# Moving the loads of four input sets into the second FFT stage, returning the filter taps in four parts, and re-ordering a weight conversion

## The chip, the cores and the metric

One core of a Trainium2 chip runs the whole kernel. The metric is the time of one execution on the device, in microseconds; the time before is the median of three runs. The engines are PE (TensorE matmul, with its weight loads PEld), DVE (VectorE), ACT (ScalarE), POOL (GpSimd) and SP (SyncE), which here issues every DMA.

## The reference

Three layers follow one another on 12480 tokens of 128 channels. The first is a long convolution in the sequence with a generated filter, gated by x; the second and third are feed-forward layers of width 2048.

```
h = (relu(pos_emb @ w1) @ w2) * exp(-0.01 * pos)     # filter taps, 12480 x 128
u = x * v
y = irfft(rfft(u, 2S) * rfft(h, 2S))[:S]             # causal convolution, every channel
x1 = x * y
h1 = x1 @ w_in                                       # 128 -> 2048
x2 = (P(h1) / (Q(h1) + 1e-6)) @ w_out                # P cubic, Q quadratic in h1
out = leaky_relu(x2 @ w2_in) @ w2_out
```

The weights of the two feed-forward layers (`ws`, four matrices) come as 64-bit floats and are converted on the chip.

## The kernel before, in words

The transform of length 2S is done in two stages of matmuls (a split of the index by 128), for two groups of 64 channels, g = 0 and 1. The kernel goes through these stages in order; every engine gets its instructions in the order of the Python text, and works them off in that order.

1. The filter net (`layer1`, `layer2`) makes the taps: those of group 0 stay in `hf` (a part of the tile `wk`), those of group 1 go to a DRAM buffer `hsc`.
2. The first stage of group 0: 16 steps `first(0, 1, i)` on the taps, then 16 steps `first(0, 0, i)` on u. Each step is 16 matmuls (L555) into one of three PSUM buffers (`bank_b`), and one ACT copy into `A` (L561).
3. The second stage of group 0, `second_stage(0)`: NB = 23 blocks, each with a table of 256 KB from DRAM (`c_m`, L570, four buffers `mt`, loaded three blocks ahead). A block is 8 forward matmuls (`xp`, L587), an ACT copy (L589), two DVE products (L596), two DVE sums (L602, L603), and, three blocks later, 8 inverse matmuls (`gp`, L622), an ACT copy (L635) into one of two `gs` buffers and a store to the DRAM buffer `bd` (L642). The last three inverse halves alternate with the first steps of the next stage.
4. The first stage of group 1: 16 steps on u, 16 on the taps, which are read back from `hsc` into `hf` (L313, L315).
5. The second stage of group 1, where POOL does the sums.
6. The two-layer part: 26 tiles of tokens, in an order that a planner writes out (`plan`); every matrix product of both layers and of the last transform step is in it.

u is made in 16 sets of 8 channels, sets 0 to 7 for group 0, 8 to 15 for group 1. `load_x` puts x of a set at u's own place, `load_v` puts v into one of four buffers `VS`, and `make_u` multiplies (L398) and forms sum and difference (L400), then issues the loads of v four sets on and of x six sets on. Two sets are made in stage 1, twelve in stage 2, two in stage 3 (blocks 0 and 2).

The conversion of the weights goes through 16 pieces of 512 columns (`conv_w`), 512 KB of DRAM each, with two buffers `raw`, which lie where two of the `VS` buffers were. It is a generator: `feed(n)` issues the next n steps, one DVE instruction each. A piece has six steps (L506 exponent, L509 sign, L512 mantissa, L517 low word, L521 sign and exponent merged, L525 product) and, for the first eight pieces, a seventh (L533, the low part of a split, after ACT's L530 has made the high part). ACT's Relu on the exponent (L507) is issued right behind L506. With the sixth step the load of the piece two on is issued (L494). 28 steps fall in stage 3 (from block 4 on), 64 in stage 4, the rest in stage 5. The loads of pieces 0 and 1 stand between stages 2 and 3.

All DMAs go through SP's one queue in the order of the text; an issue whose buffer isn't free holds up what is behind it.

Of the kernel before, what the change touches and what calls it, by code (L numbers as in the profile page):

```python
# [10 lines left out]
F32 = mybir.dt.float32  # L11
F32R = mybir.dt.float32r
# [282 lines left out]
def conv_moe_moe(ctx: ExitStack, tc: tile.TileContext, I, out, dbg=None):  # L295
# [13 lines left out]
    def spread(eng, dst, src):  # L309

        n = dst.shape[0]
        m = n // 16 * 16
        eng.dma_start(dst[:m], src[:m])  # L313
        if m < n:
            eng.dma_start(dst[m:], src[m:])  # L315

    with tc.manual_schedule():
# [61 lines left out]
        VB = 4  # L379
        VS = [cut(wk, N2 * DG + i * 2 * DS * 64, [DS, 2, N2 // 2]) for i in range(VB)]  # L380
        pool.memset(cone, C1)

        act.activation(pars[:, 6:7], cone, AF.Abs_reciprocal_sqrt)
# [3 lines left out]
        def load_x(c):  # L387
            if c < NG * NS:
                sp.dma_start(u[c // NS][:96, c % NS], I["xu"][c, :96])

        def load_v(c):
            if c < NG * NS:
                spread(sp, VS[c % VB][:NU], I["vu"][c])

        def make_u(c):

            t, w = u[c // NS][:NU, c % NS], VS[c % VB][:NU]
            dve.tensor_tensor(out=w, in0=w, in1=t, op=ALU.mult)  # L398
            for q, alu in ((0, ALU.add), (1, ALU.subtract)):
                dve.tensor_tensor(out=t[:, :, q], in0=w[:, :, 1], in1=w[:, :, 0], op=alu)  # L400
            load_v(c + VB)
            load_x(c + VB + 2)

        sp.dma_start(w1b, I["w1b"])
        for a, b in zip(PJ, PJ[1:]):
# [93 lines left out]
        def conv_w(c):  # L499
            k, q = divmod(c, NQ)  # L500
            l, sl = k % 2, slice(q * QW, (q + 1) * QW)
            raw = raws.pop(c)
            hi, lo = raw[:, :, 1], raw[:, :, 0]
            ex, sc = (view(t, [QW], I32) for t in ("ex", "sc"))
            w = view("w", [QW]) if k < 2 else uw[:, l * FF + q * QW : l * FF + (q + 1) * QW]
            dve.tensor_scalar(out=ex, in0=hi, scalar1=0x7FF00000, scalar2=None, op0=ALU.bitwise_and)  # L506
            act.activation(ex, ex, AF.Relu, bias=-float(896 << 20))  # L507
            yield
            dve.tensor_scalar(out=sc, in0=hi, scalar1=-0x80000000, scalar2=None, op0=ALU.bitwise_and)  # L509
            yield  # L510

            dve.tensor_scalar(  # L512
                out=hi, in0=hi, scalar1=0xFFFFF, scalar2=0x100000, op0=ALU.bitwise_and, op1=ALU.bitwise_or
            )
            yield
            w0 = hi.bitcast(F32)
            dve.scalar_tensor_tensor(  # L517
                out=w0, in0=lo.bitcast(U32), scalar=2.0**-32, in1=hi, op0=ALU.mult, op1=ALU.add
            )
            yield  # L520
            dve.scalar_tensor_tensor(  # L521
                out=sc, in0=ex, scalar=3, in1=sc, op0=ALU.logical_shift_left, op1=ALU.bitwise_or
            )
            yield
            dve.scalar_tensor_tensor(  # L525
                out=w, in0=w0, scalar=-(2.0**-20) if k == 2 else 2.0**-20, in1=sc.bitcast(F32), op0=ALU.mult, op1=ALU.mult
            )
            load_w(c + 2)
            if k < 2:
                act.copy(wh[l][:, sl], w)  # L530
            yield
            if k < 2:
                dve.tensor_tensor(out=wl[l][:, sl], in0=w, in1=wh[l][:, sl].bitcast(F32), op=ALU.subtract)  # L533
                yield

        def conv_all():
            for c in range(4 * NQ):
# [137 lines left out]
        for i in range(16):  # L675
            first(0, 0, i)
            if i < 3:
                run(st, 1)
            if i in (1, 4, 7, 10, 13):
                make_u(uc)  # L680
                uc += 1
        load_w(0)
        load_w(1)
        ustack.close()
        wpool = ctx.enter_context(tc.tile_pool(name="wpool", bufs=1, side="right", reuse_waits="tile"))
        wh = [wpool.tile([128, FF], F32R, name=f"wh{l}") for l in range(2)]
        wl = [wpool.tile([128, FF], F32R, name=f"wl{l}") for l in range(2)]
        for b in range(NB):
            run(st, 1)
            if b in (0, 2):  # L690
                make_u(uc)
                uc += 1
            if b > 3:
                feed(1 + b % 2)
        for i in range(16):
            first(1, 0, i)
            if i < 3:
                run(st, 1)
            elif i == 3:
                for c in range(0, DG, 16):  # L700
                    spread(sp, hf[:NH, c : c + 16], hsc[:, c : c + 16])
            feed(2)
        for i in range(16):
            first(1, 1, i)
# [21 lines left out]
        for b in range(NB + 3):  # L726
            run(st, 1)
            feed(1)
            if b == 17:
# [2 lines left out]
                sp.dma_start(xt0, I["xm"][:, : COLS[0]])  # L732
                load_b(bt0, 0, 0, TILES[0])
        run(st, 1)
        fstack.close()


# [274 lines left out]
```

## Time and profile before

| | |
|---|---|
| median of three runs | 1588.57 us (1585.23 to 1590.54) |
| the profiled execution | 1586.99 us, span 1585.2 us |
| mean granted TensorE clock | 0.987 |
| PE busy | 1539.4 us, 97% |
| DVE, ACT, POOL busy | 1422.8, 1315.2, 1279.8 us |
| DMA | 88.86 MB, mean 56 GB/s |

The page's slices, 40 of 39.6 us each, show where the engines are not full: the first eight slices, that is the stages 1 to 5, and the start of the last part in them.

```profile
PE   7989799799999999999999999999999999999999
DVE  6577577599999999999999999999999999999992
ACT  5523543388999999999999999999999999999995
POOL 5000037488999999999999999999999999999993
PEclk9999899699999999999999999999999999999999
DMA  8954655684011110111101000000000000000000
```

A digit is the busy share of a slice in tenths; PEclk is the granted clock in tenths of full speed, DMA the mean busy share of the 16 DMA engines.

### The profile page before, as it was taken

What the parts mean: (1) busy time and instruction counts of PE and PEld (TensorE: products, weight loads), DVE (VectorE), ACT (ScalarE), POOL (GpSimd) and SP (SyncE); (2) the same over time, 40 slices, a digit from 0 to 9 for tenths busy, and PEclk for the clock granted to TensorE, in tenths of its full rate; (3) what the DMA queues carried; (4) which work ended last, traced back from release to release, by engine and by line L of the source; (5) the groups of instructions that cost most, each with busy time, mean ns of one, the idle gap of its engine ahead of it and who ended that gap; (6) DMA issues with size and microseconds to landing.
All of it is one profiled execution on the core that took longest, in us unless ns stands there. A gap on an engine that the chain in (4) does not pass through costs nothing.

```text
span 1585.2 us, 21639 instructions
## 1 busy us (share of the span) xinstructions
PE 1539.4 (97%) x6782; PEld 1078.3 (68%) x6782; DVE 1422.8 (90%) x2426; ACT 1315.2 (83%) x2532; POOL 1279.8 (81%) x1098
## 2 busy tenths in 40 slices
PE   7989799799999999999999999999999999999999
PEld 5878688687666666666666666666666666666665
DVE  6577577599999999999999999999999999999992
ACT  5523543388999999999999999999999999999995
POOL 5000037488999999999999999999999999999993
PEclk9999899699999999999999999999999999999999
DMA  8954655684011110111101000000000000000000
GB/s 242 255 166 152 175 171 177 155 175 100 5 34 34 28 34 7 34 34 28 34 7 34 13 14 1 13 13 13 13 7 7 14 7 7 7 7 1 8 7 13
DMA packets 79849, 88.86 MB, mean 56 GB/s; under 512 B 51745, under 2 KB 59651, under 8 KB 79079
## 3 DMA queue, kind: packets, MB, share of 16 engines
q1 hardware_dynamic: 79734, 87.49, 20.2%
q8 instruction: 53, 0.87, 0.2%
q14 instruction: 62, 0.50, 0.1%
HBM read 66.59 MB, written 20.88 MB: 55 GB/s over the span
## 4 chain that ended last, share of the span: by engine, by line
PE 58%; POOL 18%; DVE 10%; DMA 7%; ACT 4%; issue 3%; SPq 0%; POOLq 0%; ACTq 0%; DVEq 0%
PE o1p L864 13%; PE o2p L864 9%; POOL wk L900 8%; PE h L424 7%; PE h L425 7%; PE h L426 7%; PE yP L818 3%; PE xp L587 3%; POOL wk L891 3%; POOL wk L893 3%; DMA wk<-vu 3%; DVE v L902 2%; PE gp L622 2%; DVE g L915 2%; DVE wk L897 2%
## 5 line engine op out<-in xcount | busy, mean ns | idle before, releaser
L900 POOL TENSOR_TENSOR wk<-wk 128x972 f32<-128x972 f32 (+2 forms) x208 | 470.5, 2262 | 40.7 <-DVE wk L897 29.7
L864 PE MATMUL o1p<-g,u 128*128 128x486 f32 (+2 forms) x832 | 384.1, 570 | 1.4 <-DVE g L915 1.1
L891 POOL TENSOR_SCALAR wk<-wk,pars 128x486 f32<-128x486 f32 (+2 forms) x416 | 314.4, 756 | 21.0 <-ACT wk L883 19.6
L902 DVE SCALAR_TENSOR_TENSOR v<-wk,absb,v 128x486 f32<-128x486 f32 (+2 forms) x416 | 297.1, 714 | 8.1 <-ACT v L885 7.5
L864 PE MATMUL o2p<-wk,u 128*128 128x486 f32 (+2 forms) x624 | 297.3, 565 | 0.0
L909 DVE SCALAR_TENSOR_TENSOR v<-v,u 128x486 f32<-128x486 f32 (+2 forms) x416 | 273.6, 658 | 12.8 <-ACT u L907 11.7
L885 ACT ACTIVATE v<-h,absb 128x486 f32<-128x486 f32 (+2 forms) x416 | 262.8, 645 | 20.0 <-DVE g L915 17.6
L897 DVE TENSOR_TENSOR wk<-h,wk 128x486 f32<-128x486 f32 (+2 forms) x416 | 270.7, 651 | 1.6 <-POOL wk L891 0.7
L912 DVE SCALAR_TENSOR_TENSOR v<-v,u 128x486 f32<-128x486 f32 (+2 forms) x416 | 262.1, 658 | 2.5
L915 DVE TENSOR_TENSOR g<-wk,v 128x486 f32<-128x486 f32 (+2 forms) x416 | 256.2, 648 | 8.1 <-POOL wk L900 6.7
L907 ACT ACTIVATE u<-u 128x486 f32<-128x486 f32 (+2 forms) x416 | 254.8, 613 | 6.9
L922 ACT ACTIVATE wk<-h 128x486 f32<-128x486 f32 (+2 forms) x416 | 239.2, 576 | 23.5 <-PE h L426 12.7
L905 ACT ACTIVATE u<-v 128x486 f32<-128x486 f32 (+2 forms) x416 | 238.2, 573 | 20.1 <-DVE v L902 12.9
L424 PE MATMUL h<-zh,wh 128*128 128x486 f32 (+2 forms) x416 | 247.1, 594 | 4.5 <-ACT rh L924 3.1
L883 ACT ACTIVATE wk<-h 128x486 f32<-128x486 f32 (+2 forms) x416 | 238.7, 574 | 10.8 <-PE h L426 7.8
L893 POOL TENSOR_SCALAR wk<-wk,pars 128x972 f32<-128x972 f32 (+2 forms) x208 | 239.4, 1151 | 0.0
L424 PE MATMUL h<-uh,wh 128*128 128x486 f32 (+2 forms) x416 | 231.7, 557 | 0.7 <-DVE wk L897 0.7
L864 PEld LDWEIGHTS o1p<-g,u 128*128 128x128 f32 x832 | 153.0, 189 | 93.6 <-issue 37.2
L602 POOL TENSOR_TENSOR wk<-wk 128x256 f32<-128x256 f32 x22 | 18.2, 828 | 204.6 <-DVE wk L596 199.5
L425 PE MATMUL h<-zl,wh 128*128 128x486 f32 (+2 forms) x416 | 159.7, 384 | 0.0
L426 PE MATMUL h<-zh,wl 128*128 128x486 f32 (+2 forms) x416 | 159.2, 383 | 0.0
L425 PE MATMUL h<-ul,wh 128*128 128x486 f32 (+2 forms) x416 | 158.7, 381 | 0.0
(86 smaller groups left out, 2309.9 us busy)
## 6 DMA issues: line engine op xcount, KB each, us to landing
bd<-wk SPq DMA_DIRECT2D x44, 256.0 KB
bt<-bd SPq DMA_DIRECT2D x100, 112.5 KB
wk<-c_m SPq DMA_DIRECT2D x43, 256.0 KB
dt<-c_d SPq DMA_DIRECT2D x25, 344.5 KB
wk<-ws SPq DMA_DIRECT2D x16, 512.0 KB
u<-xu SPq DMA_DIRECT2D x16, 384.0 KB
wk<-vu SPq DMA_DIRECT2D x16, 384.0 KB
xt<-xm SPq DMA_DIRECT2D x13, 243.0 KB
```

The source lines that it names most:

```text
L424: pe.matmul(dst, w_h, z_h, start=start, stop=False)
L425: pe.matmul(dst, w_h, z_l, start=False, stop=False)
L426: pe.matmul(dst, w_l, z_h, start=False, stop=stop)
L864: pe.matmul(o, wo[l][:, f], T.pop((src, n))[:, :w], start=(f == 0), stop=(f == NF - 1))
L885: act.activation(bank("v", n)[:, :w], one("h1"), AF.Abs, scale=kk)
L891: pool.tensor_scalar(out=q, in0=sq, scalar1=a3, scalar2=a1, op0=ALU.mult, op1=ALU.add)
L893: pool.tensor_scalar(out=new("p", n, 2)[:, : 2 * w], in0=T["s", n][:, : 2 * w], scalar1=a2, scalar2=a0, op0=ALU.mult, op1=ALU.add)
L897: dve.tensor_tensor(out=half("nn"), in0=one("h1"), in1=two("q"), op=ALU.mult)
L900: pool.tensor_tensor(out=nn, in0=nn, in1=T["p", n][:, : 2 * w], op=ALU.add)
L902: dve.scalar_tensor_tensor(out=one("v"), in0=two("s"), scalar=bb, in1=one("v"), op0=ALU.mult, op1=ALU.add)
L909: dve.scalar_tensor_tensor(out=one("v"), in0=one("v"), scalar=C1, in1=one("r0"), op0=ALU.add, op1=ALU.mult)
L915: dve.tensor_tensor(out=mk("g"), in0=two("nn"), in1=one("v"), op=ALU.mult)
```

## The change

Only sets 0 to 11 are made before the second stage of group 0. Of the last four sets, x and v load in its blocks 0 to 10, v into two new buffers `VL` (where later the second layer's low weights lie), and u is formed one DVE instruction a block, in blocks 4 to 15. The weights' first two loads are issued in blocks 8 and 9, and the conversion starts at block 11, with one step a block. A conversion piece has five DVE steps and, for the split pieces, a sixth, which is issued inside the next piece; ACT's two steps are issued later too: the Relu behind the second step (on a result of the first), the copy to the high part inside the next piece. The load of the piece two on is issued one step earlier. The taps' return is issued in four parts, at steps 4, 7, 10 and 13 of the first stage of group 1 instead of all at step 3.

```diff
+        def form_u(c):
+            t, w = u[c // NS][:NU, c % NS], v_of(c)
             dve.tensor_tensor(out=w, in0=w, in1=t, op=ALU.mult)
+            yield
             for q, alu in ((0, ALU.add), (1, ALU.subtract)):
                 dve.tensor_tensor(out=t[:, :, q], in0=w[:, :, 1], in1=w[:, :, 0], op=alu)
-            load_v(c + VB)
-            load_x(c + VB + 2)
+                yield
+        def make_u(c):
+            for _ in form_u(c):
+                pass
+            if c + VB < LATE:
+                load_v(c + VB)
+            if c + VB + 2 < LATE:
+                load_x(c + VB + 2)
...
             dve.tensor_scalar(out=ex, in0=hi, scalar1=0x7FF00000, scalar2=None, op0=ALU.bitwise_and)
-            act.activation(ex, ex, AF.Relu, bias=-float(896 << 20))
+            while rest:
+                act.copy(*rest.pop())
             yield
-            dve.tensor_scalar(out=sc, in0=hi, scalar1=-0x80000000, scalar2=None, op0=ALU.bitwise_and)
+            m = w.bitcast(I32)
+            dve.tensor_scalar(
+                out=m, in0=hi, scalar1=0xFFFFF, scalar2=0x100000, op0=ALU.bitwise_and, op1=ALU.bitwise_or
+            )
+            act.activation(sc, ex, AF.Relu, bias=-float(896 << 23), scale=8.0)
             yield
-            dve.tensor_scalar(
-                out=hi, in0=hi, scalar1=0xFFFFF, scalar2=0x100000, op0=ALU.bitwise_and, op1=ALU.bitwise_or
-            )
-            yield
-            w0 = hi.bitcast(F32)
+            while lows:
+                out, a, b = lows.pop()
+                dve.tensor_tensor(out=out, in0=a, in1=b.bitcast(F32), op=ALU.subtract)
+                yield
             dve.scalar_tensor_tensor(
-                out=w0, in0=lo.bitcast(U32), scalar=2.0**-32, in1=hi, op0=ALU.mult, op1=ALU.add
+                out=w, in0=lo.bitcast(U32), scalar=2.0**-32, in1=m, op0=ALU.mult, op1=ALU.add
             )
             yield
             dve.scalar_tensor_tensor(
-                out=sc, in0=ex, scalar=3, in1=sc, op0=ALU.logical_shift_left, op1=ALU.bitwise_or
+                out=sc, in0=hi, scalar=-0x80000000, in1=sc, op0=ALU.bitwise_and, op1=ALU.bitwise_or
             )
+            load_w(c + 2)
             yield
...
-            load_w(c + 2)
             if k < 2:
-                act.copy(wh[l][:, sl], w)
+                rest.append((wh[l][:, sl], w))
+                lows.append((wl[l][:, sl], w, wh[l][:, sl]))
             yield
...
-            if i in (1, 4, 7, 10, 13):
+            if i in (2, 6, 10):
                 make_u(uc)
                 uc += 1
-        load_w(0)
-        load_w(1)
...
+        LOADS = {
+            0: [(load_x, 12)], 1: [(load_v, 12)], 2: [(load_x, 13)], 3: [(load_v, 13)], 4: [(load_x, 14)],
+            5: [(load_x, 15)], 7: [(load_v, 14)], 8: [(load_w, 0)], 9: [(load_w, 1)], 10: [(load_v, 15)],
+        }
+        late = (x for c in range(LATE, NG * NS) for x in form_u(c))
         for b in range(NB):
             run(st, 1)
-            if b in (0, 2):
-                make_u(uc)
-                uc += 1
-            if b > 3:
-                feed(1 + b % 2)
+            for load, c in LOADS.get(b, ()):
+                load(c)
+            if 4 <= b < 16:
+                run(late, 1)
+            if b >= 11:
+                feed(1)
...
-            elif i == 3:
-                for c in range(0, DG, 16):
-                    spread(sp, hf[:NH, c : c + 16], hsc[:, c : c + 16])
+            elif i in (4, 7, 10, 13):
+                c = (i - 4) // 3 * 16
+                spread(sp, hf[:NH, c : c + 16], hsc[:, c : c + 16])
             feed(2)
```

Not shown are the allocations (`VL`, the second layer's low weights in a pool of their own behind it) and a last `feed(100)` after the second stage of group 1.

## Rows read from the trace of the kernel before

**Rows 1.** Busy time by stretch: engines with instructions, granted clock, DMA share, GB/s.
```profile
74.40:91.80 17.40, 11.63 (x41) 9.21 (x42) 14.82 (x24) 2.34 (x4) 0.00 (x0) 0.80 0.71 200
91.80:156.90 65.10, 63.73 (x293) 55.01 (x291) 49.11 (x98) 25.07 (x44) 0.00 (x0) 1.00 0.50 158
...
169.00:215.50 46.50, 38.76 (x465) 34.62 (x464) 30.70 (x58) 27.89 (x42) 0.00 (x0) 0.89 0.67 185
...
293.00:1585.20 1292.20, 1278.80 (x4776) 856.81 (x4776) 1223.05 (x2082) 1187.64 (x2313) 1208.27 (x1012) 0.99 0.11 26
```

**Rows 2.** The chain that ended last: start us, us, what.
```profile
79.13 6.59 DMA wk<-c_m
...
170.44 6.91 DMA wk<-hsc
...
177.42 11.15 DMA wk<-ws
```

**Rows 3.** PE's timeline, 74 to 97 us: start, us, instruction, idle before.
```profile
74.44 3.72 PE L587 MATMUL xp<-A,wk 128*128 128x256 f32 x16 [0.92 <-ACT A L561]
...
85.86 3.75 PE L587 MATMUL xp<-A,wk 128*128 128x256 f32 x8 [4.55 <-DMA wk<-c_m]
...
91.77 1.89 PE L587 MATMUL xp<-A,wk 128*128 128x256 f32 x8
93.50 1.89 PE L622 MATMUL gp<-wk,em 128*128 128x256 f32 x8
95.22 1.89 PE L587 MATMUL xp<-A,wk 128*128 128x256 f32 x8
```

**Rows 4.** PE's timeline, the first stages of both groups and the last block.
```profile
53.83 19.69 PE L555 MATMUL ap<-f,u 98*64 98x180 f32 x256
...
156.06 1.03 PE L587 MATMUL xp<-A,wk 128*128 128x256 f32 x4
...
169.00 13.64 PE L555 MATMUL ap<-f,u 98*64 98x180 f32 x176
190.38 5.07 PE L555 MATMUL ap<-f,u 98*64 98x180 f32 x32 [7.74 <-ACT A L561]
195.23 20.32 PE L555 MATMUL ap<-f1t,wk 128*64 128x180 f32 x256
```

**Rows 5.** SP's timeline, the issue of the first two weight pieces.
```profile
76.15 2.89 SPq L494 DMA_DIRECT2D wk<-ws  x2
```

**Rows 6.** SP's waits, 0 to 220 us: total us, times, longest.
```profile
SPq L494 <- DVE wk L525: 22.7, 6, 4.8
```

**Rows 7.** Busy time by stretch, three stretches with full DMA engines; columns as rows 1.
```profile
50.00:75.00 25.00, 24.09 (x313) 22.24 (x310) 17.64 (x21) 15.19 (x20) 0.00 (x0) 1.00 1.04 246
...
130.00:135.00 5.00, 5.00 (x24) 4.12 (x23) 3.73 (x8) 2.42 (x5) 0.00 (x0) 1.00 0.91 330
175.00:187.00 12.00, 7.64 (x102) 6.88 (x96) 4.52 (x8) 4.44 (x7) 0.00 (x0) 0.97 1.02 225
```

**Rows 8.** Groups of instructions, 74.4 to 216 us: busy us, mean ns, idle before.
```profile
L521 DVE SCALAR_TENSOR_TENSOR wk<-wk 128x512 int32<-128x512 int32 x14 | 9.6, 687 | 3.5 <-ACT wk L507 3.5
...
L507 ACT ACTIVATE wk<-wk 128x512 int32<-128x512 int32 x14 | 8.9, 633 | 12.9 <-DVE wk L506 12.9
...
L509 DVE TENSOR_SCALAR wk<-wk 128x512 int32<-128x512 int32 x14 | 5.9, 421 | 0.0
...
L398 DVE TENSOR_TENSOR wk<-wk,u 98x1024 f32<-98x1024 f32 x3 | 3.7, 1223 | 3.3 <-DMA wk<-vu 3.3
```

**Rows 9.** The page's DMA issues: count, KB each.
```profile
bd<-wk SPq DMA_DIRECT2D x44, 256.0 KB
...
wk<-c_m SPq DMA_DIRECT2D x43, 256.0 KB
...
wk<-ws SPq DMA_DIRECT2D x16, 512.0 KB
...
wk<-vu SPq DMA_DIRECT2D x16, 384.0 KB
...
wk<-hsc SPq DMA_DIRECT2D x4, 640.0 KB
```

More of the change, by code (lines that the diff above doesn't have):

```diff
@@ L378, in conv_moe_moe, with v_of @@
         w2n, w1n = (win[:, : N2 // 2], win[:, N2 // 2 : N2]), win[:, N2:]
-        VB = 4
+        VB, LATE = 4, 12
         VS = [cut(wk, N2 * DG + i * 2 * DS * 64, [DS, 2, N2 // 2]) for i in range(VB)]
+        VL = []
+        def v_of(c):
+            return (VS[c % VB] if c < LATE else VL[c % 2])[:NU]
         pool.memset(cone, C1)
@@ L392, in load_v @@
             if c < NG * NS:
-                spread(sp, VS[c % VB][:NU], I["vu"][c])
-        def make_u(c):
-            t, w = u[c // NS][:NU, c % NS], VS[c % VB][:NU]
+                spread(sp, v_of(c), I["vu"][c])
+        def form_u(c):
+            t, w = u[c // NS][:NU, c % NS], v_of(c)
             dve.tensor_tensor(out=w, in0=w, in1=t, op=ALU.mult)
+            yield
             for q, alu in ((0, ALU.add), (1, ALU.subtract)):
                 dve.tensor_tensor(out=t[:, :, q], in0=w[:, :, 1], in1=w[:, :, 0], op=alu)
-            load_v(c + VB)
-            load_x(c + VB + 2)
+                yield
[6 more added lines that the diff above has]
+                load_x(c + VB + 2)
         sp.dma_start(w1b, I["w1b"])
@@ L521, in conv_w @@
             dve.scalar_tensor_tensor(
-                out=sc, in0=ex, scalar=3, in1=sc, op0=ALU.logical_shift_left, op1=ALU.bitwise_or
+                out=sc, in0=hi, scalar=-0x80000000, in1=sc, op0=ALU.bitwise_and, op1=ALU.bitwise_or
             )
+            load_w(c + 2)
             yield
             dve.scalar_tensor_tensor(
-                out=w, in0=w0, scalar=-(2.0**-20) if k == 2 else 2.0**-20, in1=sc.bitcast(F32), op0=ALU.mult, op1=ALU.mult
+                out=w, in0=w, scalar=-(2.0**-20) if k == 2 else 2.0**-20, in1=sc.bitcast(F32), op0=ALU.mult, op1=ALU.mult
             )
-            load_w(c + 2)
             if k < 2:
-                act.copy(wh[l][:, sl], w)
+                rest.append((wh[l][:, sl], w))
+                lows.append((wl[l][:, sl], w, wh[l][:, sl]))
             yield
-            if k < 2:
-                dve.tensor_tensor(out=wl[l][:, sl], in0=w, in1=wh[l][:, sl].bitcast(F32), op=ALU.subtract)
-                yield
+        rest, lows = [], []
         def conv_all():
@@ L678, in conv_moe_moe @@
                 run(st, 1)
-            if i in (1, 4, 7, 10, 13):
+            if i in (2, 6, 10):
                 make_u(uc)
                 uc += 1
-        load_w(0)
-        load_w(1)
         ustack.close()
+        tstack = ExitStack()
         wpool = ctx.enter_context(tc.tile_pool(name="wpool", bufs=1, side="right", reuse_waits="tile"))
         wh = [wpool.tile([128, FF], F32R, name=f"wh{l}") for l in range(2)]
-        wl = [wpool.tile([128, FF], F32R, name=f"wl{l}") for l in range(2)]
+        wl = [wpool.tile([128, FF], F32R, name="wl0")]
+        vpool = tstack.enter_context(tc.tile_pool(name="vpool", bufs=1, side="right", reuse_waits="tile"))
+        VL += [vpool.tile([128, DS, 2, N2 // 2], F32, name=f"vl{i}") for i in range(2)]
+        assert uc == LATE
+        LOADS = {
[3 more added lines that the diff above has]
+        late = (x for c in range(LATE, NG * NS) for x in form_u(c))
         for b in range(NB):
             run(st, 1)
-            if b in (0, 2):
-                make_u(uc)
-                uc += 1
-            if b > 3:
-                feed(1 + b % 2)
+            for load, c in LOADS.get(b, ()):
[4 more added lines that the diff above has]
+                feed(1)
+        tstack.close()
+        l1pool = ctx.enter_context(tc.tile_pool(name="l1pool", bufs=1, side="right", reuse_waits="tile"))
+        wl.append(l1pool.tile([128, FF], F32R, name="wl1"))
         for i in range(16):
@@ L734, in conv_moe_moe @@
         run(st, 1)
+        feed(100)
         fstack.close()
```

## The prediction

> **What bounds the kernel now.** I read four views, in this order. The stretch table of all engines comes first: it cuts the run at the stages that the kernel's text names. From 293 us on, in the two-layer part, PE is busy 1278.80 of 1292.20 us [rows 1]; the change touches nothing there, so this part only shifts in time. Ahead of it, PE is busy 11.63 of the 17.40 us at the start of the second stage of channel group 0 (74.4 to 91.8), nearly all of 91.8 to 156.9, and 38.76 of 46.50 us in the first stage of group 1 (169 to 215.5). In both of the loose stretches the granted clock is below 1.00 as well, which is time at the lower of its two levels. So the question is what PE waits for at these two places.
>
> The chain of waits answers it, and the reader is to see three entries in it [rows 2]: 6.59 us for a table block (`wk<-c_m`) issued at 79.13, then 6.91 us for hf (`wk<-hsc`) from 170.44, and 11.15 us for a piece of weights (`wk<-ws`) issued at 177.42. All three are transfers on the one SP queue.
>
> PE's own timeline gives sizes [rows 3]. The second stage starts at 74.44 with two blocks at once; the fourth block starts at 85.86, after 4.55 us of idleness that a `c_m` load ended, and its eight matmuls take 3.75 us where eight take 1.89 later: it is the half clock. From 91.77 on a block comes every 95.22 - 91.77 = 3.45 us, half of it the forward matmuls (`xp`) and half the inverse ones (`gp`), eight of one shape each: 1.73 us a half. In the first stage of group 1, PE stops before 190.38 for 7.74 us because ACT doesn't copy, and ACT doesn't copy because its next instruction, the weights' Relu, waits for VectorE, which waits for the weights [rows 2, 4].
>
> The SP issues say why the table block was late: in the queue's order it stands behind x and v of the sets up to 15 and behind two 512 KB weight pieces, which go out from 76.15 on [rows 5], so its own issue is at 79.13 [rows 2].
>
> **The change, part by part.**
>
> *1. Loads of x and v for sets 12 to 15 and of weight pieces 0 and 1 leave the first stage.* That is 4 x (384 + 392) KB + 2 x 512 KB, 4.2 MB (a v load is its 384 KB and a tail of 8 KB) [rows 9]. At the 246 GB/s that the DMA engines gave there at a share of 1.04, that is fully busy [rows 7], it is 17 us of transfers that are no longer ahead of the tables. PE itself is busy 24.09 of 25 us in that stretch, so the end of the first stage at 74.4 doesn't move. Tables 0 to 3 and x of set 12 have nothing to wait for on the queue and land before 74. The stretch from 74.44 to the fifth block then costs three lone `xp` halves, one `xp` with its `gp`: 5 x 1.73 = 8.65 us, and the fifth block starts at 83.1 instead of 91.77. Gain: 91.77 - 74.44 - 8.65 = **8.7 us**. Next late would be table 4, which waits for the first block's matmuls (76.2) and has until 83.1; it needs about 1 us of transfer. Bounds: 8.7 if it is in time, about 5 if tables 4 and 5 come behind x and v at two or so us each.
>
> *2. The same loads, now inside the second stage.* In steps 0 to 10 there is one more transfer in nearly each step. Prices: 256 KB of tables or of stores at 330 GB/s, which a busy share of 0.91 gave, so some 360 at full share [rows 7, 9]; I take 330, 0.79 us. One x or v: 384 KB at 246/1.04 = 237 GB/s, 1.66 us. A weight piece: 1.59 us. Between 76.2 and the end of step 10 (83.1 + 7 x 3.45 = 107.3) the queue carries ten tables and eight stores (18 x 0.79 = 14.2), seven x and v (11.6; x of set 12 is earlier) and two weight pieces (3.2): 29.0 us of work in 31.1 us. It fits, with 7% to spare. Tables have three steps of lead, and a store has until its buffer returns two steps later. SP is blocked less: a weight load waits on VectorE's conversion step that stands behind the whole block, 22.7 us in six times [rows 6], and holds the tables and stores queued after it. Four such loads fell between 91.77 and 156.06, now two do (the other two wait for nothing). From the fifth block to the last at 156.06 there are 18 steps, 62.1 us, so these blocks cost 2.1 us now [rows 3, 4]; I keep half of that and add 0.6 for the fuller queue. Gain: **0.5 us**. Bounds: +2.1 to -4.8 us, the latter if all of it goes at the 237 GB/s of x and v (35.9 us for 31.1).
>
> *3. Forming u of these sets on VectorE in steps 4 to 15.* One instruction a step, 1.22 us the longest [rows 8]. A step has 49.11/65.10 x 3.45 = 2.6 us of VectorE work now, a conversion instruction of about 0.5 in it [rows 1, 8]; with 1.22 in its place some 3.3 us in 3.45; no instruction of the path comes later by more than that 1.2, and a block's PSUM has three buffers. I cost it at nothing; if the cover fails it costs four times about 1 us.
>
> *4. hf comes back in four parts, and weights go between them.* Today 4 x 656 KB (640 and a tail of 16) [rows 9] stand as one lump ahead of a weight piece, hence 11.15 us. From 169.00 to the end of the first stage of group 1 (195.23 + 20.32 = 215.55) PE has 29 steps; sixteen such steps took 19.69 us in group 0, 1.23 each, so it needs 35.7 us, and takes 46.5 [rows 4]. So 10.8 us are lost, 7.74 of them idle and the rest at the half clock. After: every three steps (3.7 us) one part and one weight piece share the queue, (672 + 524) kB at the 225 GB/s of just this mixture [rows 7]: 5.3 us, 1.6 too much, four times 6.4. The first excess is hidden by the two raw buffers, so VectorE comes about 4.5 us late in all, and PE may run two steps (2.5 us) ahead of ACT's copies. I take 2.0 us lost, in small pieces that don't drop the clock. Gain: **8.8 us**. Bounds: 10.8 (nothing late) to 2 (each excess reaches PE, with the clock falling as now).
>
> The Trainium skill's page "SBUF — State Buffer", section "Summary: rules for kernel authors", says to estimate a transfer between HBM and SBUF with about 358 GB/s. By it a part and a weight piece would take 3.3 us and fit their 3.7, and the sum would be 2.0 us better. The row of this very mixture disagrees, 225 GB/s at a share of 1.02 [rows 7].
>
> *5. Conversion.* One VectorE instruction (L509) of 0.42 us a piece goes, 16 in all. The others have the shapes and engines of rows that are there: sign mask and merge as the 0.69 us one, the Relu 0.63 us [rows 8]. None is on PE's path unless its weights are late: the saving is worth nothing by itself. ACT's Relu and copy now wait on VectorE results that are a step old, so that ACT doesn't stand behind VectorE; that is in the sums of 2 and 4. The 12 last conversion steps fall in the second stage of group 1, as before. Its last weight load now waits on VectorE in that stage's first step and holds table 4 there: I take 0, with +-1.5.
>
> **Sum.** 8.7 + 0.5 + 8.8 = 18.0 us. The profiled execution took 1586.99 us with a span of 1585.2; less 18.0 it is 1569.0. The median of the runs shown, 1588.57, lies 1.6 us above that execution, which is inside their own spread of 1585.23 to 1590.54. I forecast 1569.
>
> **Rivals.**
>
> *A. hf still gets in the way.* The wait for weights is spread over four places instead of removed: all 6.4 us reach PE and the clock falls (some 3 us). Loss 9 instead of 2: gain 11, 1576. For it: these transfers fill the queue (1.02). Against: each delay is under two steps. Chance 0.15.
>
> *B. The second stage becomes bound by transfers, mildly.* Part 2 comes to its -4.8 us and part 1 loses 3: gain 5.7 - 4.8 + 8.8 = 9.7, 1577. For: 7% to spare only. Against: lead of three steps. Chance 0.12.
>
> *C. Slower.* The second stage doesn't get beyond the rate that it shows now, 158 GB/s [rows 1]. From 76.2 to its last block, at 146 by my sum, it must carry 19 tables, 23 stores, seven x and v, four weight pieces: 15.8 MB in 70 us, 226 GB/s. At 158 this takes 100 us; 30 lost against 18.0 won, 1599. It decides below 15.8 / (70 + 18) = 180 GB/s, where stores come back too late for the two `gs` buffers, ACT waits and PE behind it. Against it: the 158 come at a share of 0.50 [rows 1], the queue stands idle half of the time. Chance 0.07.
>
> *D. No change.* The same at about 180 GB/s: 1585 to 1592. Chance 0.05.
>
> **How the numbers follow.** The forecast has 0.61, with 1564 to 1574 as its own range (all losses gone: 8.7 + 2.1 + 10.8 + 1.5 = 23.1; at the other end a gain of 13). A and B reach 1577, both together 1581. The range is 1562 to 1581. About 0.3%, 4.8 us, is what a measurement here can tell from no change: faster 0.88 (forecast, A, B), within 0.05 (D), slower 0.07 (C).
>
> **What would show it.** Right: no `c_m` wait of PE between 74 and 92 and the fifth block's `xp` near 83; block step 3.45 to 3.6 us through step 10 with a DMA share near 0.9; the first stage of group 1 in 36 to 39 us with granted clock 1.00; the two-layer part as long as now. Part 1 is wrong if PE waits for a table in steps 3 to 5; part 2 if ACT's copies of `gp` wait for `bd` stores in most steps up to 10; part 4 if VectorE's first conversion instruction waits for `ws` over 2 us at a time and PE behind it. The whole is wrong if the two-layer part changes by over 2 us.

## The result, and the profile after

The changed kernel takes 1575.44 us (median of 8 runs, 1572.51 to 1582.58), the kernel before 1588.57 (8 runs, 1585.23 to 1594.53): ratio 0.9915, interval [0.990, 0.993]. That is 13.1 us won; 18.0 were forecast (1569, range 1562 to 1581). The profiled execution took 1575.34 us, mean granted clock 0.989.

Two rows of the changed kernel's page (span 1573.6 us), in slices of 39.3 us:

```profile
PE   7999999799999999999999999999999999999999
...
PEclk9999999699999999999999999999999999999999
```

PE's third slice (the start of the second stage of group 0) and its fifth (the first stage of group 1) read 9 now, where they read 8 and 7, and the clock's fifth is back at 9 too. The first (the filter net) and the eighth (the start of the two-layer part) stay low. PE's own timeline says where the time went (start in us, duration, instruction, idle before it):

```profile
77.00 7.17 PE L602 MATMUL xp<-A,wk 128*128 128x256 f32 x32 [0.91 <-ACT A L576]
...
85.73 1.89 PE L602 MATMUL xp<-A,wk 128*128 128x256 f32 x8
...
133.80 1.99 PE L637 MATMUL gp<-wk,em 128*128 128x256 f32 x8 [1.28 <-ACT wk L650]
...
149.44 1.03 PE L602 MATMUL xp<-A,wk 128*128 128x256 f32 x4
...
161.33 16.08 PE L570 MATMUL ap<-f,u 98*64 98x180 f32 x208
179.14 2.66 PE L570 MATMUL ap<-f1t,wk 128*64 128x180 f32 x32 [1.73 <-ACT A L576]
...
184.38 2.66 PE L570 MATMUL ap<-f1t,wk 128*64 128x180 f32 x32 [0.93 <-ACT A L576]
...
195.57 6.32 PE L570 MATMUL ap<-f1t,wk 128*64 128x180 f32 x80 [0.78 <-ACT A L576]
202.80 5.45 PE L602 MATMUL xp<-A,u 128*128 128x256 f32 x24 [0.91 <-ACT A L576]
```

The second stage of group 0 opens with 32 `xp` matmuls in a row and no wait for a table: 85.73 - 77.00 = 8.73 us to the fifth block, 91.77 - 74.44 = 17.33 before [rows 3]. The blocks then run at PE's own pace but for one stop of note, before 133.80. In the first stage of group 1 the one long stop of 7.74 us, with the half clock behind it [rows 4], has become five short ones at full clock. The table of stretches (length, then busy time of PE, PEld, DVE, ACT, POOL, granted clock, DMA share, GB/s) shows it as clock and transfer rate:

```profile
77.00:85.70 8.70, 8.70 (x40) 7.69 (x41) 5.74 (x12) 2.35 (x4) 0.00 (x0) 1.00 0.66 202
85.70:149.40 63.70, 62.42 (x289) 54.63 (x289) 52.17 (x98) 22.57 (x39) 0.00 (x0) 1.00 0.61 191
161.30:202.80 41.50, 36.74 (x465) 32.71 (x464) 30.21 (x55) 29.41 (x46) 0.00 (x0) 1.00 0.83 219
...
280.90:1573.60 1292.70, 1280.46 (x4776) 858.44 (x4776) 1223.46 (x2082) 1187.72 (x2313) 1208.14 (x1012) 0.99 0.11 26
```

The clock is 1.00 in the three stretches of the change (0.80, 1.00 and 0.89 before [rows 1]), and the second stage moves 191 GB/s instead of 158. In the first stage of group 1 PE still needs only 36.74 of 41.50 us.

The same cuts of PE's timeline for this kernel and for all kernels below (us, each of one profiled execution; "first": up to the first step on the taps; "st1": the first stage of group 0; "to 5th" and "blocks": its second stage up to the start of the fifth block, and from there to the start of the last; "to u": to the fourth step on u of group 1, the first that no inverse half interrupts; "1st g1": from there to the second stage of group 1; "2nd g1": up to its last inverse half; "to w": to the two-layer part's first matmul; "two-layer": from there to the end):

| kernel | first | st1 | to 5th | blocks | to u | 1st g1 | 2nd g1 | to w | two-layer | span |
|---|---|---|---|---|---|---|---|---|---|---|
| before | 34.26 | 40.18 | 17.33 | 64.29 | 12.94 | 47.41 | 72.75 | 5.85 | 1290.19 | 1585.2 |
| after | 35.33 | 41.67 | 8.73 | 63.71 | 11.89 | 41.47 | 71.40 | 6.69 | 1292.71 | 1573.6 |
| loads_only | 35.30 | 40.18 | 8.74 | 64.55 | 11.86 | 47.00 | 79.64 | 5.86 | 1291.47 | 1584.6 |
| loads_only_28 | 35.16 | 41.73 | 8.73 | 70.11 | 11.86 | 47.57 | 72.12 | 5.92 | 1290.30 | 1583.5 |
| taps_only | 34.77 | 42.17 | 14.99 | 64.51 | 12.93 | 39.39 | 72.76 | 5.88 | 1291.50 | 1578.9 |
| conversion_only | 34.95 | 40.17 | 17.29 | 63.50 | 11.86 | 46.87 | 70.02 | 5.94 | 1295.00 | 1585.6 |
| without_late_loads | 35.04 | 40.17 | 17.85 | 63.57 | 11.85 | 43.12 | 69.97 | 6.65 | 1296.98 | 1585.2 |
| lump_back | 35.29 | 40.17 | 8.74 | 63.71 | 11.85 | 47.20 | 71.38 | 6.73 | 1296.63 | 1581.7 |
| no_taps_return | 36.93 | 41.85 | 8.74 | 63.53 | 11.85 | 36.46 | 71.45 | 6.73 | 1295.76 | 1573.3 |
| more_steps_early | 34.26 | 40.18 | 8.74 | 66.14 | 11.86 | 38.26 | 71.18 | 5.85 | 1296.83 | 1573.3 |
| more_early_and_held | 35.03 | 41.85 | 8.74 | 62.16 | 11.90 | 38.05 | 71.18 | 5.78 | 1290.11 | 1564.8 |
| held_weights | 36.23 | 41.74 | 8.73 | 62.17 | 11.85 | 38.10 | 71.18 | 6.81 | 1297.09 | 1573.9 |
| taps_five_apart | 37.84 | 41.66 | 8.74 | 63.69 | 11.90 | 42.51 | 71.41 | 6.72 | 1290.63 | 1575.1 |
| held_and_five_apart | 37.02 | 41.85 | 8.74 | 62.16 | 11.86 | 38.32 | 71.17 | 5.93 | 1290.25 | 1567.3 |

From before to after, the five columns from "to 5th" to "2nd g1" fall by 8.60 + 0.58 + 1.05 + 5.94 + 1.35 = 17.5 us. The other columns, in whose matmuls nothing is changed, grow by 1.07 + 1.49 + 0.84 + 2.52 = 5.9. The span gained the rest, 11.6. So two things are to be explained: why the first stage of group 1 gave 5.94 and not 8.8, and what the 5.9 are.

In the second stage what is left is SP. Its timeline (start, time on SP):

```profile
121.12 0.33 SPq L657 DMA_DIRECT2D bd<-wk  x1
126.60 0.33 SPq L506 DMA_DIRECT2D wk<-ws  x1
...
127.50 0.38 SPq L657 DMA_DIRECT2D bd<-wk  x1
```

For 5.1 us, from the end of the store of 121.12, SP stood at the weight load of 126.60, which waits on VectorE; the tables and stores behind it came in a bunch, and the store of 127.50 took 5.56 us to land (chain below). ACT, which needs that store's buffer, held PE before 133.80.

To the first question the waits of the changed kernel from 158 to 215 us lead (total, times, longest):

```profile
ACT wk L526 <- DVE wk L518: 9.6, 8, 2.1
DVE wk L518 <- DMA wk<-ws: 8.9, 6, 3.0
...
PE ap L570 <- ACT A L576: 3.9, 5, 1.7
```

and the transfers behind them stand in its chain (start, duration, what):

```profile
127.50 5.56 DMA bd<-wk
...
168.52 8.80 DMA wk<-ws
...
179.95 6.44 DMA wk<-ws
...
189.01 4.75 DMA wk<-ws
...
195.90 3.77 DMA wk<-ws
```

VectorE waits 8.9 us for weight pieces, ACT behind it 9.6, and PE 3.9 behind ACT. A piece took 3.77 us from issue to landing where nothing is left ahead of it (195.90), 8.80 and 6.44 where a part of the taps is (168.52, 179.95), and 4.75 behind two tables and `em` that SP issued from 185.62 on (189.01; the fourth part had gone out at 174.06).

### The profile page after: what moved, and what is told of

Its sections match the earlier page's. It is cut to its first block, busy times and chain, and to the rows that moved or that the text cites. A ratio compares the mean times of both kernels' runs of the same rounds, so it can differ in the third digit from the quotient of the medians.

```text
span 1573.6 us, 21619 instructions
## 1 busy us (share of the span) xinstructions
PE 1537.9 (98%) x6782; PEld 1077.8 (68%) x6782; DVE 1415.5 (90%) x2410; ACT 1315.3 (84%) x2532; POOL 1280.2 (81%) x1098
## 4 chain that ended last, share of the span: by engine, by line
PE 64%; POOL 16%; DVE 9%; ACT 3%; issue 3%; DMA 2%; SPq 0%; POOLq 0%; ACTq 0%; DVEq 0%
PE o1p L891 13%; PE o2p L891 10%; POOL wk L927 8%; PE h L436 7%; PE h L437 7%; PE h L438 7%; PE xp L602 4%; PE yP L845 4%; PE ap L570 3%; POOL wk L918 3%; POOL wk L920 3%; PE gp L637 2%; DVE v L929 2%; DVE g L942 2%; DVE wk L924 2%
## 5 line engine op out<-in xcount | busy, mean ns | idle before, releaser
L910 ACT ACTIVATE wk<-h 128x486 f32<-128x486 f32 (+2 forms) x416 | 238.7, 574 | 11.6 <-PE h L438 8.3
```

## The experiments

The theory for the first stage of group 1: parts of the taps and weight pieces share one queue, pieces land late, and PE stops behind ACT and VectorE. The rival: the weights are late without the taps too, since a piece's load is issued only when one of two buffers is free. For the second stage the question was what the late loads are worth, and what the rest of the stops there are.

**One part of the change at a time.** Loads only (the kernel after with the old conversion and hf's lump; of the 28 old conversion steps of the second stage, 18 stay and the others go to the second stage of group 1):

```diff
-                    if b >= 11: feed(1)
+                    if b >= 11: feed(1 + b % 2)
...
-                elif i in (4, 7, 10, 13): ...one part of hf...
+                elif i == 3:
+                    for c in range(0, DG, 16): spread(sp, hf[...], hsc[...])
```

> The late loads alone: x and v of sets 12 to 15 and the first weight pieces go into the second stage as in the changed kernel, but the conversion keeps its old steps (18 of them in the second stage of group 0, so that it ends in time) and the taps return in one lump at step 3. Theory Q (each gain is a wait on SP's one queue): from the second stage's first block to its fifth 8.7 us as in the changed kernel (17.3 before), the first stage of group 1 as slow as before (45 to 48 us from its third step to the second stage of group 1; 47.4 before), time 8 to 10 us under before, 1578.5 to 1580.5. Rival V (the conversion's new order, with ACT no longer behind VectorE, carries the gain): under 3 us faster than before.

Measured 1588.96 against 1590.04: 0.9991 [0.9981, 1.0001], nothing to be seen. The start of the second stage gains its 8.6 us ("to 5th"), but the second stage of group 1 takes 79.64 where 72.75 stood: two old steps in each of its first eight blocks cost 6.9 us. That cost is this kernel's own, so the run alone can't say what the loads are worth.

Taps only, on the kernel before, and conversion only, on the kernel before:

```diff
-                elif i == 3: for c in range(0, DG, 16): spread(sp, hf..., hsc...)
+                elif i in (4, 7, 10, 13):
+                    c = (i - 4) // 3 * 16; spread(sp, hf..., hsc...)
```

> The kernel before with the taps' return in four parts and nothing else. Theory Q: first stage of group 1 from 47.4 to 41 to 43 us, the start of the second stage still 17.3 us, time 4 to 6 us under before, 1582.5 to 1584.5. Rival V: the old conversion with its Relu behind VectorE keeps PE waiting, 45 us or more, under 2 us faster.

1583.48 against 1590.04: 0.9948 [0.9933, 0.9963]. The first stage of group 1 falls from 47.41 to 39.39 us, more than in the kernel after. An old piece of the first eight has seven steps, at two a PE step one piece in 3.5 steps; a new one has six, so the new conversion asks for its loads at shorter intervals. That this is the reason is likely, not shown: no run changes the interval alone. But without_late_loads, which has the same four parts and the new conversion, took 43.12 us in this stage, and VectorE's wait there (165 to 212 us; taps_only first, without_late_loads second) rose with it:

```profile
DVE wk L506 <- DMA wk<-ws: 4.0, 3, 2.9
...
DVE wk L506 <- DMA wk<-ws: 10.3, 7, 3.4
```

> The kernel before with the new conversion steps (one VectorE step less a piece, ACT's steps later, the load one step earlier) and nothing else; the number of steps issued in each stage is the old one, so it ends 16 steps sooner. Theory Q: 0 to 2 us faster, 1586.5 to 1588.5, the start of the second stage 17.3 us, first stage of group 1 45 to 48 us. Rival V: 5 us faster or more, 1583 or less.

1585.25 against 1590.04: 0.9971 [0.9958, 0.9984], 4.8 us where 0 to 2 were expected. By the table 0.8 us in the blocks, 1.1 behind them, 0.5 in the first and 2.7 in the second stage of group 1, which has no conversion steps left.

**What the first stage of group 1 waits for.** The kernel after without the read of the taps (group 1's taps are then whatever lies in hf, so the convolution of group 1 is not computed):

```diff
-                elif i in (4, 7, 10, 13): ...one part of hf...
```

> The changed kernel without the taps' return (the four transfers are left out, so the taps of group 1 are not the right ones): what the transfers cost in the first stage of group 1, which takes 41.5 us from its third step to the second stage of group 1 where 36.5 are PE's work. Theory Q (taps and weights fill the queue together): 36.5 to 38 us, time 4 to 6 us under the changed kernel, 1569.5 to 1571.5. Rival L (a weight piece's load is issued too late for two buffers, whatever else is on the queue): 40 us or more, within 2 us of the changed kernel.

1572.19 against 1590.04: 0.9879 [0.9861, 0.9897]. The stage takes 36.46 us, and PE's timeline has no stop in it up to the next stage at 199.36:

```profile
162.90 16.08 PE L570 MATMUL ap<-f,u 98*64 98x180 f32 x208
178.81 19.69 PE L570 MATMUL ap<-f1t,wk 128*64 128x180 f32 x256
```

Its waits from 160 to 200 us hold the same entry as above, at a twelfth:

```profile
DVE wk L518 <- DMA wk<-ws: 0.7, 2, 0.4
```

So the weights are nearly in time by themselves, and the rival falls. The 41.47 - 36.46 = 5.0 us between the two profiled executions are the taps' doing.

The lump put back into the kernel after, and the late loads taken out of it (which is conversion only, with the taps in four parts):

> The changed kernel with the taps' return back in one lump at step 3. Theory Q (taps and weights share one queue; a lump puts all four parts ahead of one weight piece): first stage of group 1 46 to 48 us instead of 41.5, the fifth block still 8.7 us behind the first, 5 to 7 us slower than the changed kernel, ratio to the kernel before 0.994 to 0.997. Rival V (with ACT's steps later the lump no longer stops PE): under 43 us, within 2 us of the changed kernel.

> The kernel before with the taps in four parts and the new conversion, without the late loads (28 conversion steps are issued in the second stage of group 0 as before, 12 in the changed kernel). Theory M (the 16 conversion steps that the late loads push out of the second stage cost the later stages about what the late loads win): fifth block 15 to 17.3 us behind the first, but first stage of group 1 38 to 39.5 us and second stage of group 1 70 to 70.5 us; within 3 us of the changed kernel, ratio to before 0.990 to 0.9935. Rival W (the late loads are worth their 8.7 us in the whole): 6 to 9 us slower than the changed kernel, ratio 0.995 to 0.997.

With the lump 1579.11 against 1588.99: 0.9939 [0.9923, 0.9954], the stage at 47.20, with one stop of PE:

```profile
180.73 5.71 PE L570 MATMUL ap<-f,u 98*64 98x180 f32 x48 [8.55 <-ACT A L576]
```

Without the late loads 1582.14: 0.9954 [0.9936, 0.9971]. Beside the whole change (0.9915 [0.990, 0.993]), the four parts are worth 0.24%, 3.8 us (the two intervals touch; by the stage it is 47.20 - 41.47 = 5.7 us), the late loads 0.39%, about 6 us, with intervals apart. That the late loads net nothing, as theory M and the first run had it, is refuted: without them the first stage of group 1 took 43.12 us, not the expected 38 to 39.5.

**What is left in the second stage.** A second run of the loads alone, now with all 28 old steps kept, two a block from block 9 (weights' loads in blocks 5 and 6, the last v in block 10):

> The late loads alone once more, with the old conversion steps issued as the kernel before has them: 28 in the second stage of group 0 (two a block from block 9, weight pieces 0 and 1 loaded in blocks 5 and 6), 64, and 12 in the second stage of group 1 (loads_only had over 22 there, which cost 7 us). Theory Q: fifth block 8.7 us behind the first, from the fifth to the last block 64 to 66.5 us, first stage of group 1 46 to 48, second stage 72.5 to 73; ratio to before 0.9945 to 0.997. Rival W (the loads only move the wait): ratio 0.998 or more.

1587.79 against 1589.89: 0.9988 [0.9974, 1.0003], again nothing, which is the rival's number but not its reason: the start still gains 8.6 us, and the blocks take 70.11 instead of 64.29 (64 to 66.5 expected). Its waits from 88 to 162 us:

```profile
ACT wh L542 <- DVE wk L537: 11.3, 4, 4.2
```

The old piece's two ACT instructions are issued right behind the VectorE result that they read, so ACT stands behind VectorE (4.2 us once), with PE's copies queued after it. All 28 old steps packed into the last fourteen blocks cost 5.8 us, ten of them moved to the second stage of group 1 cost 6.9. Of the ways tried, the late loads paid only beside the new conversion.

Then the kernel after with more new steps early, which starts the conversion at block 7:

```diff
-        5: [(load_v,14)], ..., 8: [(load_w,0)], 9: [(load_w,1)], 10: [(load_v,15)]
+        5: [(load_w,0)], 6: [(load_w,1)], 7: [(load_v,14)], 8: [(load_x,15)], 9: [(load_v,15)]
-                    if b >= 11: feed(1)
+                    if b >= 7: feed(1 + (b >= 16))
...
-                feed(2)
+                feed(2 - i % 2)
```

The last two lines stand in the first stage of group 1, in its steps on u.

With `load_v(15)` in block 9, v of set 15 lands before the last instruction on set 13 has read their common buffer, so set 13's difference is formed of set 15's v; amount and order of the work are the same, and the times can be read. The next kernel shares this.

> The changed kernel with the conversion started at block 7 of the second stage of group 0 (weight pieces 0 and 1 load in blocks 5 and 6, x and v of set 15 in 8 and 9): 23 steps there, and 24 instead of 32 in the steps on u of the first stage of group 1, in which the taps return. Theory M: first stage of group 1 37.5 to 39.5 us instead of 41.5, second stage of group 0 up to 1 us longer (four weight loads instead of two hold SP), second stage of group 1 no longer than 71.4; 1.5 to 3 us under the changed kernel, ratio 0.9895 to 0.991. Rival D (VectorE or the DMA queue has no room for 11 more steps in the second stage): its blocks take 2 us or more longer in all, no faster than the changed kernel.

1575.12 against 1588.99: 0.9899 [0.9883, 0.9915], not clearly apart from the kernel after. The first stage of group 1 falls to 38.26 (24 steps instead of 32 in its part on u, so fewer pieces meet the taps), but the blocks rise to 66.14, by 2.4 us where at most 1 was expected. Two explanations stood: SP held by the two further weight loads, each of which waits on VectorE's step of its own block (Q), or 512 KB ahead of the tables on the DMA engines (G). The next kernel leaves the bytes as they are and issues each weight load one block later, when VectorE is done or nearly so:

```diff
-            load_w(c + 2)
+            held.append(c + 2)
...
-                    feed(1 + (b >= 16))
+                    flush()           # issues what is held
+                    feed(1 + (b >= 16), hold=b < NB - 1)
```

> more_steps_early, and in the second stage of group 0 each weight load is issued one block later, behind that block's table and store, so that SP never waits there for the VectorE step that frees the buffer. Theory Q: from the fifth block to the last 62.2 to 62.8 us (63.7 in the changed kernel, 62.1 is PE's own work), about 1 us faster than more_steps_early. Rival G (the stores come late because 512 KB are ahead of them, not because SP waits): 63.5 us or more.

1567.95 against 1588.99: 0.9875 [0.9855, 0.9895]. The blocks take 62.16, which is 18 steps of 3.453 us, PE's own time. With the same bytes nothing is left, so G falls: it was SP standing behind VectorE, 66.14 - 62.16 = 4.0 us, and 63.71 - 62.16 = 1.55 us in the kernel after. SP's own waits from 84 to 150 us, more_steps_early first, this kernel second:

```profile
SPq L506 <- DVE wk L536: 13.3, 3, 6.0
...
SPq L506 <- DVE wk L536: 4.7, 3, 2.7
```

The cost isn't spread evenly over the loads. In more_steps_early nearly all of it is one stop, behind the first load (PE idle for 3.47 us before 119.62, SP held for 6.0 us until 111.20); in the kernel after it is the stop before 133.80, also behind the first load, while the second (147.90) cost nothing up to the last block.

The same with `load_v(15)` in block 10, so that set 13 keeps its own v:

> more_early_and_held with v of set 15 loaded one block later (in block 10), so that set 13 is formed of its own v. Theory Q: as more_early_and_held, 62.2 us from the fifth block to the last, first stage of group 1 38.1 us; ratio to before 0.986 to 0.9895, under the changed kernel by 5 to 8 us.

1572.55 against 1589.89: 0.9893 [0.9874, 0.9912], by the ratios 0.2% (3.5 us, where 5 to 8 were expected) under the kernel after and no better than more_steps_early; the stages are as expected, the blocks again 62.17 (86.70 to 148.87) and the first stage of group 1 38.10.

**The taps further apart**, five steps between parts instead of three, the fourth in step 3 (counted from 0) on the taps:

```diff
-                elif i in (4, 7, 10, 13): c = (i - 4) // 3 * 16; ...
+                elif i in (4, 9, 14): c = (i - 4) // 5 * 16; ...
...
+            if i == 3: spread(sp, hf[:NH, 48:64], hsc[:, 48:64])
```

The last line stands in the steps on the taps.

> The changed kernel with the four parts of the taps' return five steps apart (4, 9, 14 of the steps on u, 3 of those on the taps) instead of three. Theory Q (a part and a weight piece need 5.3 us together, more than three steps of PE and less than five): first stage of group 1 38 to 39.5 us instead of 41.5, 2 to 3.5 us under the changed kernel, ratio to before 0.9895 to 0.9905. Rival L2 (a weight piece's own time from issue to landing binds, whatever is ahead of it): 41 us or more, no faster.

1577.16 against 1589.89: 0.9932 [0.9912, 0.9951]; the stage took 42.51 us, and the expected gain didn't come. PE's timeline says why:

```profile
163.83 16.08 PE L570 MATMUL ap<-f,u 98*64 98x180 f32 x208
179.74 13.59 PE L570 MATMUL ap<-f1t,wk 128*64 128x180 f32 x176
197.49 8.00 PE L570 MATMUL ap<-f1t,wk 128*64 128x180 f32 x80 [4.15 <-ACT A L576]
```

For the first three parts it ran 29.5 us without a stop (163.83 to 193.3), as expected. The stop came with the fourth. SP's issues (start, time on SP):

```profile
183.51 0.83 SPq L585 DMA_DIRECT2D u<-c_m  x2
184.38 0.43 SPq L313 DMA_DIRECT2D wk<-hsc  x1
185.47 0.51 SPq L737 DMA_DIRECT2D em<-c_e  x1
186.35 17.89 SPq L506 DMA_DIRECT2D wk<-ws  x5
```

I had put it among the tables of the next stage and `em`, all ahead of the next piece; VectorE waited 4.24 us for that piece, PE 4.15, and the clock fell with it: the next 80 matmuls took 8.00 us, 6.32 in the kernel after. The table of stretches (columns as above):

```profile
197.50:206.30 8.80, 7.99 (x80) 6.77 (x80) 7.92 (x16) 6.15 (x10) 0.00 (x0) 0.81 0.51 149
```

The queue explains this too, but the run doesn't show that five apart is better. The stage came out as rival L2 has it (41 us or more); its reason, that a piece's own time binds whatever is ahead, doesn't fit the 29.5 us without a stop, nor no_taps_return.

Both together:

> held_weights with the taps' parts five steps apart. Theory Q: first stage of group 1 36.5 to 37.5 us (36.46 is what it took without the taps' return), about 1 us under held_weights, ratio to before 0.985 to 0.989.

1567.56 against 1589.89: 0.9859 [0.9838, 0.9881], the fastest that computes the whole of it, 22 us below before and below the kernel after (0.9915). Its first stage of group 1 is no shorter than with three apart (38.32 against 38.10; 36.5 to 37.5 were expected), so the gain over the kernel after is the held loads and the earlier steps. Between it and held_weights the profiled executions differ by 6.6 us, and all of that lies in the two-layer part (next section); that the 5 us between their medians have the same cause is likely, not shown.

## Why the prediction was right in kind and its gain 4.9 us too high

*Part 1, 8.7 us: right.* 8.60 measured; the fifth block's `xp` came 8.73 us after the first one, and no kernel with the late loads has a `c_m` wait there.

*Part 2, 0.5 us: right in size.* 0.58. Of the 1.65 us kept as lost (half of 2.1, and 0.6 for the fuller queue) 1.55 are there, all of it the first cause: SP behind VectorE, gone in the held kernels. The fuller queue cost nothing: the loads of x and v are in all kernels with 62.16. From the fifth block through step 10 the DMA share was 0.83, at 256 GB/s.

*Part 3, nothing: right* while the conversion gives way; with two old conversion steps a block beside them these steps had no room (5.8 us, loads_only_28), with one and two in turn from block 11 on the blocks stayed about as before (64.55, loads_only).

*Part 4, 8.8 us: the term that failed.* "I take 2.0 us lost": 5.0 were lost (41.47 against 36.46 without taps; 36 to 39 was to be seen). The bound of 10.8 was right (47.41 - 36.46 = 10.95), the clock stayed at 1.00 as forecast, and the mechanism is the one of the sum, pieces late behind parts of the taps. The size went wrong at "VectorE comes about 4.5 us late in all": it waited 8.9. Nor was "the first excess" hidden: for the four pieces issued behind parts VectorE waited 1.85, 2.99, 1.94 and 0.53 us, for two later ones 1.55. I counted only the 1.6 us by which a part and a piece exceed their slot, as if the queue's work alone set the landing. But a piece needs 3.77 us from issue to landing even with nothing ahead, and it is issued only when a buffer comes free; with a part ahead it was 6.44 and 8.80, and two buffers didn't hide that. PE stopped five times behind it, 3.9 us in all. By the prediction's own sign, a wait of VectorE for `ws` over 2 us with PE behind it (the longest was 3.0), part 4 was wrong. The Trainium skill's page "SBUF — State Buffer", section "Summary: rules for kernel authors", takes about 358 GB/s for such transfers; by that rate alone a piece is an estimate of 1.5 us. The 3.77 us here, from issue to landing, are longer.

*Part 5, 0 with 1.5 either way: inside its bounds, but not for its reason.* The second stage of group 1 gained 1.35. That "the saving is worth nothing by itself" did not hold: conversion_only won 4.8 us. "to u" gained 1.05, which no term had. It comes with the conversion alone and with the loads alone (11.86 in both): in the kernel before, PE stopped for 1.01 us before 164.61, when ACT waited for a `bd` store that stood behind a weight load on SP (158.70).

By stages the sum is 17.5 for 18.0, errors of part 4 (-2.9) and of the small terms (+2.4) against each other; that it comes out so near is luck. The time itself, 1575.44, lies inside the range but outside the 1564 to 1574 that the forecast gave itself. Two of the prediction's sums don't come out: A and B together leave 18.0 - 7.0 - 8.3 = 2.7 us of gain, 1584 and not 1581, and the traffic of C is too high, 13.9 MB (202 GB/s for 8.7 us, 191 for 63.7) and not 15.8 up to the last block. Neither changed the outcome.

*What the prediction had no place for:* the 5.9 us in columns that the change doesn't touch. It said that the whole would be wrong if the two-layer part changed by over 2 us; it changed by 2.52. The profiles show two places where executions differ, and not by what was changed. One is the first stage of group 0: 40.17 or 40.18 us in six profiles, 41.66 to 42.17 in eight. PE is thin just before it. Stretches of the kernel before (the stage begins at 34.26):

```profile
30.00:34.00 4.00, 2.01 (x32) 1.55 (x29) 3.93 (x5) 2.34 (x5) 1.52 (x1) 1.00 0.90 217
34.26:38.26 4.00, 4.00 (x52) 3.77 (x54) 3.97 (x6) 1.59 (x3) 0.00 (x0) 1.00 0.88 250
```

and of the kernel after at the same phase (it begins at 35.33):

```profile
31.10:35.10 4.00, 2.00 (x16) 1.63 (x16) 3.97 (x5) 2.37 (x5) 0.59 (x1) 0.56 0.82 214
35.33:39.33 4.00, 4.00 (x34) 3.31 (x36) 3.93 (x5) 0.76 (x1) 0.00 (x0) 0.62 0.96 285
```

In the first of these rows PE does 32 matmuls in 2.01 us, in the third 16 in 2.00: the clock stays at 1.00 in the one execution and falls to 0.56 in the other. The four us ahead of them are alike (40 matmuls in 2.61 and 2.59 us, clock 1.00), and so are the two stops (1.39 and 0.67 us). The kernel before and taps_only, whose text is the same up to the first stage of group 1, differ here too: the last sixteen matmuls of the filter net start at 31.57 and 31.58 and take 1.10 and 1.60 us, and the stage behind them takes 40.18 and 42.17. The other place is the start of the two-layer part: 1290.1 to 1292.7 us in eight profiles, 1295.0 to 1297.1 in six. Stretches of held_weights, whose two-layer part begins at 276.81:

```profile
296.00:306.00 10.00, 9.50 (x36) 8.22 (x36) 6.43 (x16) 4.70 (x12) 5.22 (x6) 0.50 0.32 71
306.00:316.00 10.00, 9.02 (x38) 7.57 (x37) 4.82 (x12) 4.99 (x14) 6.00 (x8) 0.67 0.89 207
```

and the same stretches of held_and_five_apart, where it begins at 277.05:

```profile
296.00:306.00 10.00, 8.91 (x62) 7.99 (x62) 8.62 (x22) 6.98 (x17) 7.85 (x9) 0.98 0.57 140
306.00:316.00 10.00, 9.12 (x64) 7.79 (x63) 8.66 (x22) 7.23 (x19) 8.01 (x10) 1.00 0.96 211
```

There the first runs at a clock of 0.50, the lower level throughout, and issues 36 matmuls where the second issues 62 at 0.98. 1297.09 against 1290.25 is all of their difference in span (6.6 us). The 2.52 us from before to after arise here too, nearly all of them between the 160th and the 200th matmul, 34 to 43 us behind the part's start. For the first 30 us the two executions are alike (34, 43 and 64 matmuls in 10 us each, the clock at 0.50, 0.50, and 0.95 or 0.98); in the next 10 (before first, after second) the clock dips only in the kernel after:

```profile
325.00:335.00 10.00, 9.40 (x63) 8.17 (x64) 9.16 (x23) 7.64 (x21) 8.22 (x11) 1.00 0.95 212
...
310.90:320.90 10.00, 8.83 (x53) 7.74 (x54) 8.07 (x20) 6.07 (x16) 6.66 (x8) 0.87 0.96 209
```

So of the 5.9 us most is clock: this, the 1.49 in the first stage of group 0, and 0.90 in the last matmuls of the filter net (1.10 us before, 2.00 after). The rest is open. The kernel before was at the short end in both places in its profiled execution, and at 1586.99 us that execution was 1.6 to 3 us under the medians of its runs (1588.57 to 1590.04), so a sum taken from it was that much too favourable. Whether the change makes such losses likelier stays open: the first stage of group 0 was long in one of four profiles with the old loads of x and v and in seven of ten with the late ones, the two-layer part in two of four and four of ten; no run here decides it.

*The rivals.* A is what happened by its mechanism, with 5.0 us of loss between its 9 and the forecast's 2, without the fall of the clock. B's loss in part 2 did not come; the second stage carried 191 GB/s (C's point was 180) with PE busy 62.42 of 63.70 us. D is out.

*The parts alone and together.* Alone 0.1, 0.5 and 0.3%, together 0.85%: the sums agree, the members don't. The late loads are worth 0.1% alone (not clear of noise) and 0.4% beside the new conversion; the parts of the taps 0.5% alone and 0.24% beside it, likely since shorter pieces ask for their loads sooner.

## What to carry to other kernels

When a transfer is cut up to share a queue with a stream of loads, price each load by its time from issue to landing behind the piece ahead, not by the excess of bytes over the slot, and compare that with what the stream's buffers hold. On a queue that issues in order, put a load whose buffer has just been read one block later: waits of 5 and 6 us of SP on VectorE cost PE 1.55 and about 3.7 us here, and nothing when the loads were deferred. Work that is displaced by a move (the old conversion's steps) must be priced where it lands.

## What the runs showed of the hardware that was not expected

- Whether the clock falls in one and the same thin stretch differs from execution to execution, and the times form groups: 1.5 to 2 us apart at the first stage of group 0, about 6 us (medians 1290.5 and 1296.7) in the two-layer part. Differences of 0.3% between kernels here need several executions of each, and a look at such places in the profile.
- Busy DMA engines moved unlike amounts: 246 GB/s at a share of 1.04 for x and v (96 partitions), 225 at 1.02 for the taps (80) with weights, 330 at 0.91 for tables and stores of 128 [rows 7]. That the partitions are the reason isn't shown; direction and row length differ as well.
- A load of 512 KB with nothing ahead of it took 3.77 us from issue to landing (195.90 in the kernel after), 139 GB/s over that time: the DMA share was 0.00 in its first 0.5 us, and 0.73 with 240 GB/s from 197 to 199.
